# Block 0's second query half evicted by ScalarE, and block 14's last rows, a router product and a guard step in other places

## The chip, the cores and the metric

One core of one Trainium2 chip runs the whole kernel. The metric is device microseconds (us) of one launch. Five engines run beside each other and meet through semaphores: TensorE (PE in the profile) multiplies, VectorE (DVE) and ScalarE (ACT) read PSUM and write SBUF, GpSimd (POOL) works on SBUF and starts indirect DMAs, SyncE (SP) starts the other DMAs.

## The reference

Input x is 2048 tokens of 448 numbers (bfloat16). The first half is attention with 16 heads of 28 numbers, one shared key and one shared value head. The second half is a mixture-of-depths MLP: only the 8 tokens with the largest router value go through it.

```python
h  = x + attention(layernorm(x))        # q = xn @ wq (16 heads), k = xn @ wk, v = xn @ wv (one head)
                                        # softmax(q k^T / sqrt(28)) @ v, then @ wo
n  = layernorm(h)
r  = n @ w_r                            # router, one number per token
idx = argsort(-r)[:8]
y  = ((silu(n[idx] @ w_gate) * (n[idx] @ w_up)) @ w_down) * sigmoid(r[idx])
out = h + n;  out[idx] += y
```

## The kernel before

**Tiling.** Tokens are cut into 16 tiles of 128. A *block* b is a tile of 128 queries with all 16 heads, a *tile* j is 128 keys. For every pair (b, j) TensorE makes four strips of scores, 128 keys x 512 (query, head) pairs each. Of these 256 pairs, 169 go to ScalarE, which takes two strips in one `Exp` into `P` (`act_tile`, line 888; line 874 for the early tiles below, which are kept in the buffers of `wg_sb` and `wu_sb`). The other 87 go to VectorE (`dve_tile`, line 915): it clamps the scores to an int16 whose bits are an approximate exponential, `Y`, and GpSimd adds two constants to copies of it, `Yc` (line 926); three products with differently scaled values sum to the exponential. TensorE multiplies `P`, `Y` and `Yc` with the values into one PSUM bank, `ACC`, one block after the other (line 853). `_ND` is the number of VectorE tiles of each block (sum 87 before and after).

**Start.** `group(g)` handles one group of token tiles, `groups = [[0], [1], [2, 3], [4, 5], [6, 7], [8..11], [12..15]]`: layer norm statistics (lines 724 to 733), normalised rows `of` (ScalarE line 742 or VectorE lines 737 and 746), transposes to `xnT` (757, 762), keys `K` (772) and values `Vs` (785). Keys are wanted twice, in `K[:, 0]` and, shifted by 32 partitions, in `K[:, 1]`. For a group in `_KD` the second copy is made by two DMAs, for the others by a second VectorE instruction. `q_project(b)` makes the queries of a block: 16 matmuls, then an eviction that adds a one (line 803 on ScalarE, 806 on VectorE). Block 0 is evicted in two halves, the first by ScalarE, the second by VectorE. `_EARLY` lists positions inside block 0 at which three tiles of block 1 (keys 0, 1 and 2) are done ahead by ScalarE.

**After each block.** `evict(b)` copies `ACC` to `Ot` (953) and fetches the reciprocal of the row sums by way of DRAM (`l_scr`, `Rb`); `On` (966) is the normalised output; `out_proj(t)` multiplies by `wo` and adds x (`of`, 996), takes statistics (998, 999) and the router product `junk` (1001). `ln2` makes rstd on ScalarE with Ln and Exp (1012, 1014) and the output rows. Block 14 (`N1`) is alone in its `ln2` group; its router product is made there, with rstd already in it (line 1023), and its two row instructions run on ScalarE (1026 to `xn2`, 1030 to `of`).

**End.** `stage1` finds the best 8 tokens of each of the first 14 tiles and gathers those 112 rows by an indirect DMA (1127). `tail` finishes block 15 without DRAM: row sums by a shuffle (1156), reciprocal by Ln and Exp on ScalarE (1158, 1160) and `On` (1165), each in two halves; `last_rows` takes statistics (1041, 1042), rstd (1043, 1045), router product (1047), router value (1052) and rows (1058, 1060). Then: maximum and index over 368 candidates (1200, 1201), a one-hot `oh` (1208), the selected rows `xsel`, gate and up products, SiLU (1236 to 1244), down product, a gather of the 8 rows of the output (`base`, 1256), their sum `fin` (1264) and an indirect write (1267). A guard checks that all row sums lie in a sane interval (1276, 1278) and sets a flag that every engine waits for at the end; if it fails, an exact program runs.

**Order.** Each engine's order is made when the kernel is built: a list planner (`_Flow.plan`) goes over all instructions with a duration, a priority and their dependencies, and appends to each engine the one that can start soonest in its model, by priority within a window (`_WIN`). `_W`, `_LOOK`, `_LATE` and `_HOLD` are its settings; the duration in `G.op(engine, fn, duration)` is what the planner believes. On the chip the order of each engine is fixed and semaphores decide the times. `lock=True` keeps GpSimd's instructions from running beside a VectorE instruction.

Of the kernel before, what the change touches and what calls it, by code (L numbers as in the profile page):

```python
# [240 lines left out]
_KD = (1, 2, 4)  # L241
_EARLY = (0, 6, 9)
# [271 lines left out]
def _fast(nc, G, sb, ps, psb, flag, scr, rows, A_x, A_wq, A_wk, A_wv, A_wo, B_w_r, B_w_gate, B_w_up, B_w_down, out):  # L514
# [204 lines left out]
    def group(g):  # L719
# [29 lines left out]
        for a in range(t0, t1, 2):  # L749
            m = min(2, t1 - a)  # L750
            u = G.unit()

            def cut(a, ch):
                return 2 * (ch // 2) if a == 0 else 0

            def tr(k, ch, u=u, a=a, m=m):
                return lambda e: e.transpose(psb[0:CK, u.b[0], (ch * m + k) * 128:(ch * m + k + 1) * 128],  # L757
                                             of[:, a + k, ch * CK + cut(a, ch):(ch + 1) * CK + cut(a, ch)], ident[:, :])
            G.op(PE, [tr(k, ch) for k in range(m) for ch in range(NCH)], m * 4 * (150 if g == 0 else 80),
                 reads=[("of", a + k) for k in range(m)] + ["ident"], writes=[u.key], take=u)  # L760
            dst = xnT[0:CK, :, a * 128:(a + m) * 128]
            G.op(DV, lambda e, u=u, m=m, dst=dst: e.tensor_copy(
                dst, psb[0:CK, u.b[0], 0:NCH * m * 128].rearrange("p (c n) -> p c n", c=NCH)), 65 + m * 265,
                 reads=[u.key], writes=[("xnT", a + k) for k in range(m)], free=u)
# [26 lines left out]
    def q_project(b):  # L791
        war = G.readers.get(("Q", b % 3), [])
        for c in ((0, 2), (2, 4)) if b == 0 else ((0, 4),):
            u = G.unit()
            n = c[1] - c[0]
            for h in range(*c):
                G.op(PE, [mm(bank(u, c=slice((h - c[0]) * 128, (h - c[0] + 1) * 128)), wq_pad[0:CK, ch, h, :],
                             xnT[0:CK, ch, b * 128:(b + 1) * 128], ch == 0, ch == NCH - 1) for ch in range(NCH)], 470 if b == 0 else 430 if b == 1 else 235,
                     reads=[("wqp", ch) for ch in range(NCH)] + ["wq_pad", ("xnT", b)], writes=[u.key],
                     take=u if h == c[0] else None, after=war)  # L800
            src = lambda u=u, n=n: ps[:, u.b[0], 0:128 * n].rearrange("p (h n) -> p h n", n=128)
            if b == 0 and c[0] == 0:
                G.op(AC, lambda e, c=c, src=src: e.activation(Q[:, 0, c[0]:c[1], :], src(), ACT.Identity, bias=qone[:, 0:1]),
                     340, reads=[u.key, "qone"], writes=[("Qa", 0)], free=u)
            else:
                G.op(DV, lambda e, c=c, src=src: e.tensor_scalar(Q[:, b % 3, c[0]:c[1], :], src(), qone[:, 0:1], None, ALU.add),  # L806
                     60 + n * 150, reads=[u.key, "qone"], writes=[("Q", b % 3)], free=u)
# [200 lines left out]
    def ln2(ts):  # L1008
# [3 lines left out]
        G.op(AC, lambda e: e.activation(st[:, sl, 0], sv[:, :, 1], ACT.Ln, bias=ebias[:, 0:1]), 300,  # L1012
             reads=[("stf", t) for t in ts] + ["ebias"], writes=[("st0", t) for t in ts])
# [6 lines left out]
        for t in ts:  # L1020
            if t == N1:
                blk14.append(s3)
                G.op(DV, lambda e, t=t: e.scalar_tensor_tensor(junk[:, :], of[:, t, 0:D], st[:, t, 1:2], w_rb[:, :], ALU.mult,
                                                               ALU.mult, accum_out=st[:, t, 4:5]), 600,
                     reads=[("of", t), ("st1", t), "w_rb"], writes=["junk", ("st4", t)], lock=True)
                G.op(AC, lambda e, t=t: e.activation(xn2[:, 0, :], of[:, t, 0:D], ACT.Identity, bias=st[:, t, 3:4],
                                                     scale=st[:, t, 1:2]), 600,
                     reads=[("of", t), ("st1", t), ("st3", t)], writes=[("xn2", t)], prio=b_last,
                     after=G.readers.get(("xnT", NT - 1), []))
                G.op(AC, lambda e, t=t: e.activation(of[:, t, 0:D], of[:, t, 0:D], ACT.Identity, bias=st[:, t, 3:4],  # L1030
                                                     scale=st[:, t, 2:3]), 600,
                     reads=[("of", t), ("st2", t), ("st3", t)], writes=[("of", t)], prio=b_last)
# [7 lines left out]
    def last_rows(t, u, hp, stf):  # L1040
# [4 lines left out]
        G.op(AC, lambda e: e.activation(st[:, t, 1:2], st[:, t, 0:1], ACT.Exp, scale=-0.5), 200, reads=[("st0", t)],  # L1045
             writes=[("st1", t)])
# [102 lines left out]
    def tail():  # L1149
# [4 lines left out]
        for h in range(2):  # L1154
# [5 lines left out]
            G.op(AC, lambda e, sl=sl: e.activation(Rb[:, rb, sl], Rb[:, rb, sl], ACT.Exp,  # L1160
                                                       bias=-63.0 * math.log(2.0), scale=-1.0), 330,
                 reads=[("Rbh", h)], writes=[("Rbh", h)])
# [704 lines left out]
```

## Time and profile before

| | |
|---|---|
| median of 3 runs | 348.62 us (348.61 to 348.75) |
| profiled execution | 348.56 us |
| its span, first to last instruction | 346.6 us |
| outside the span | 1.96 us |
| busy PE / DVE / ACT / POOL | 318.2 / 319.4 / 325.4 / 190.8 us |
| first `Exp` of the scores starts, last one ends | 10.95 us, 326.93 us |

How to read it: three engines are busy over 90% of the span, so shares do not tell which one sets the end. Look at which engine has no idle time in a stage and whom the others wait for. In a timeline row the columns are start, length, engine, line, operation, output and input with shapes and count, and in brackets the idle time before it with what ended that time. Neighbouring instructions overlap by about 0.1 us in these lengths. Three stages matter: the start, until ScalarE has a full stream of `Exp` work (0 to 17 us), the stream (17 to 327 us), and the end (327 to 346.6 us).

### The profile page before, as it was taken

Reading aid. Unit: us, or ns where it says so; the run is one execution under the profiler, and the core shown is the slowest. Engines: PE = TensorE matmul, PEld = TensorE weight load, DVE = VectorE, ACT = ScalarE, POOL = GpSimd, SP = SyncE. Lnnn points to the kernel's source line nnn. Section 1 sums busy time; section 2 is a strip of 40 time slices with the busy share of each in tenths; the row PEclk is TensorE's granted clock in tenths of the full one; section 3 lists DMA queues with packets and bytes.
Section 4 is the critical chain, followed back from the end, with each engine's and each line's share of the span. In section 5 each row is a group of like instructions: output and inputs, shape, how many; then the busy total and the mean of one; then the engine's idle time right before and its main releaser. Section 6 shows DMA issues by size and latency. Waiting matters only on the chain.

```text
span 346.6 us, 8725 instructions
## 1 busy us (share of the span) xinstructions
PE 318.2 (92%) x3630; PEld 105.2 (30%) x3630; DVE 319.4 (92%) x662; ACT 325.4 (94%) x387; POOL 190.8 (55%) x206
## 2 busy tenths in 40 slices
PE   3889899999999999999999998999999999999974
PEld 2644232323232322323232322323232322222334
DVE  6998997999988999999899899999999899999874
ACT  5599999999999999999999999999999999999850
POOL 8010475666545648667456566576747456775401
PEclk9999999999999999999999999999999999999995
DMA  6510000000020205020020206020101012152210
GB/s 158 138 40 3 0 3 18 20 17 18 5 85 4 84 4 168 27 60 30 8 80 5 84 4 165 4 46 16 33 4 30 7 58 85 42 152 58 60 36 9
DMA packets 18374, 16.18 MB, mean 47 GB/s; under 512 B 6574, under 2 KB 15438, under 8 KB 18330
## 3 DMA queue, kind: packets, MB, share of 16 engines
q1 hardware_dynamic: 16826, 15.01, 15.5%
q8 instruction: 29, 0.48, 0.6%
q10 hardware_dynamic: 1392, 0.45, 0.6%
q0 software_dynamic: 112, 0.12, 0.1%
q14 instruction: 15, 0.12, 0.1%
HBM read 11.78 MB, written 3.71 MB: 45 GB/s over the span
## 4 chain that ended last, share of the span: by engine, by line
ACT 83%; DVE 9%; DMA 3%; PE 3%; issue 0%; POOLq 0%; POOL 0%; ACTq 0%; DVEq 0%
ACT P L888 80%; DVE Y L915 4%; PE ps L628 2%; DMA wqx<-in_A_wq_dram 1%; ACT wg_sb L874 1%; DMA wqx<-n_rows,cidx 1%; DVE bn L724 1%; PE ps L823 1%; DMA cidx<-gidx 1%; ACT wu_sb L874 1%; DVE K L772 0%; ACT wqx L711 0%; DVE Q L806 0%; PE ps L757 0%; DVE gidx L1123 0%
## 5 line engine op out<-in xcount | busy, mean ns | idle before, releaser
L888 ACT ACTIVATE P<-ps 128x1024 bf16<-128x1024 f32 x332 | 306.8, 1287 | 0.0
L926 POOL INT64_ADD Yc<-Y x174 | 178.5, 1037 | 127.7 <-DVE Y L915 112.3
L915 DVE TENSOR_SCALAR Y<-ps 128x512 int16<-128x512 f32 x348 | 220.0, 683 | 12.0 <-PE ps L823 11.3
L823 PE MATMUL ps<-Q,K 32*128 32x512 bf16 (+1 forms) x1024 | 147.1, 386 | 14.1 <-ACT P L888 10.8
L823 PEld LDWEIGHTS ps<-Q,K 32*128 32x128 bf16 (+1 forms) x1024 | 37.7, 91 | 142.9 <-ACT P L888 122.1
L853 PE MATMUL ps<-Yc,Vs 128*32 128x512 bf16 x696 | 63.9, 385 | 0.0
L853 PE MATMUL ps<-P,Vs 128*32 128x512 bf16 x664 | 59.4, 387 | 0.0
L853 PE MATMUL ps<-Y,Vs 128*32 128x512 bf16 x348 | 34.2, 384 | 0.2 <-DVE Ot L953 0.2
L853 PEld LDWEIGHTS ps<-P,Vs 128*32 128x32 bf16 x664 | 14.1, 93 | 28.3 <-issue 26.2
L853 PEld LDWEIGHTS ps<-Yc,Vs 128*32 128x32 bf16 x696 | 15.7, 94 | 21.5 <-issue 15.8
L628 PE MATMUL ps<-xnT,wqx 112*128 112x128 bf16 x256 | 21.6, 229 | 0.0
L628 PE MATMUL ps<-wo_pad,On 128*32 128x448 bf16 (+1 forms) x244 | 18.1, 358 | 1.2 <-DVE Y L915 0.6
L628 PEld LDWEIGHTS ps<-xnT,wqx 112*128 112x128 bf16 x256 | 15.6, 102 | 7.7 <-issue 4.8
L806 DVE TENSOR_SCALAR Q<-ps,qone 128x512 bf16<-128x512 f32 (+1 forms) x16 | 11.6, 727 | 1.0 <-PE ps L628 0.9
L853 PEld LDWEIGHTS ps<-Y,Vs 128*32 128x32 bf16 x348 | 9.1, 94 | 9.3 <-issue 7.4
L966 DVE TENSOR_TENSOR On<-Ot,Rb 128x512 bf16<-128x512 f32 x15 | 11.0, 734 | 0.5 <-DMA Rb<-l_scr 0.5
L757 PE MATMUL ps<-ident,of 128*112 128x128 bf16 x64 | 6.3, 248 | 5.5 <-DVE of L737 5.5
L996 DVE TENSOR_TENSOR of<-ps,x_sb 128x448 bf16<-128x448 f32 x15 | 9.3, 619 | 1.1 <-PE ps L628 1.1
L953 DVE COPY Ot<-ps 128x512 f32<-128x512 f32 x15 | 10.3, 685 | 0.0
L724 DVE BATCH_NORM_STATS2 bn<-x_sb 128x6 f32<-128x448 bf16 x16 | 9.5, 610 | 0.0
L998 DVE BATCH_NORM_STATS2 bn<-of 128x6 f32<-128x448 bf16 x15 | 9.3, 622 | 0.1
L1001 DVE SCALAR_TENSOR_TENSOR junk<-of,w_rb 128x448 bf16<-128x448 bf16 x14 | 8.5, 611 | 0.0
(169 smaller groups left out, 141.4 us busy)
## 6 DMA issues: line engine op xcount, KB each, us to landing
Rb<-l_scr SPq DMA_DIRECT2D x15, 256.0 KB
out_dram<-of SPq DMA_DIRECT2D x16, 112.0 KB, 2.2
n_rows<-of SPq DMA_DIRECT2D x14, 113.0 KB, 2.4
x_sb<-in_A_x_dram SPq DMA_DIRECT2D x3, 448.0 KB, 4.4
wg_sb<-in_B_w_gate_dram SPq DMA_DIRECT2D x3, 448.0 KB, 6.1
wu_sb<-in_B_w_up_dram SPq DMA_DIRECT2D x3, 448.0 KB, 6.1
xnT<-in_B_w_down_dram SPq DMA_DIRECT2D x3, 448.0 KB, 7.7
wqx<-in_A_wq_dram ACTq DMA_DIRECT2D x1, 392.0 KB, 4.6
```

The source lines that it names most:

```text
L628: return lambda e: e.matmul(o() if callable(o) else o, lhsT=l, rhs=r, start=start, stop=stop)
L724: G.op(DV, lambda e, t=t: e.bn_stats(bn6[:, t, :], x_sb[:, t, :]), 516, reads=[("x", t)], writes=[("bn6", t)], after=[G.last_w[("xnT", 0)] ...
L806: G.op(DV, lambda e, c=c, src=src: e.tensor_scalar(Q[:, b % 3, c[0]:c[1], :], src(), qone[:, 0:1], None, ALU.add), 60 + n * 150, reads=[u. ...
L823: return e.matmul(ps[:, u.b[0] + q, :], lhsT=K[a:a + w, i % 2, j * 128:(j + 1) * 128], rhs=Q[a:a + w, b % 3, :, :].rearrange("p h n -> p ( ...
L853: return e.matmul(ps[32 * i:32 * i + 32, ACC, :], lhsT=Vs[:, v, j, :], rhs=src(i), start=info["first"] == o.idx, stop=info["last"] == o.idx)
L888: G.op(AC, lambda e, u=u, p=p, n=n: e.activation(P[:, p:p + n, :], ps[:, u.b[0]:u.b[0] + n, :], ACT.Exp, bias=EB, scale=OCT), 50.0 + 426.5 ...
L915: G.op(DV, lambda e, u=u, g0=g0: e.tensor_scalar(Y0[:, g0, :].bitcast(I16), ps[:, u.b[0], :], 0.0, TOP - STEP[-1], ALU.max, ALU.min), 599, ...
L926: G.op(PO, lambda e: e.int64_add(Yc[:, c, :, :].rearrange("p a b -> p (a b)").bitcast(I64), Y0[:, 4 * s:4 * s + 4, :].rearrange("p a b -> ...
L953: o = G.op(DV, lambda e: e.tensor_copy(Ot[:, rb, :], ps[:, ACC, :]), 598, reads=[pk(ACC)], writes=[("Ot", rb)], prio=b - 10.0, after=blk[b ...
L966: G.op(DV, lambda e: e.tensor_tensor(On[:, rb, :, :].rearrange("p h n -> p (h n)"), Ot[:, rb, :], Rb[:, rb, :], ALU.mult), 599, reads=[("O ...
L996: G.op(DV, lambda e: e.tensor_tensor(of[:, t, 0:D], hp(), x_sb[:, t, :], ALU.add), 535, reads=[u.key, ("x", t)], writes=[("of", t)], free=u)
L998: G.op(DV, lambda e: e.bn_stats(bn6[:, t, :], of[:, t, 0:D]), 520, reads=[("of", t)], writes=[("bn6", t)])
```

## The change

1. In block 0 both halves of the queries are evicted by ScalarE (line 803); before, the second one went to VectorE (806).
2. `_KD` goes from groups 1, 2, 4 to groups 2, 4, 5: the shifted keys of tile 1 are written by VectorE, those of tiles 8 to 11 by DMA. `_EARLY` goes from positions 0, 6, 9 to 0, 0, 6.
3. Block 14's router product becomes the ordinary one of `out_proj` (line 1001, without rstd), and a small VectorE instruction in `tail` multiplies by rstd afterwards. Block 14's Ln (1012) must now follow the last Exp of block 15's reciprocal (1160), and block 14's two row instructions (1026, 1030) must follow block 15's rstd (1045). These are orders on ScalarE alone.
4. The second half of the guard over block 15's sums (1278) must follow the last gate product, `guT` of half 1 (1244).
5. The index addition (1123) is locked against GpSimd.
6. The planner believes shorter TensorE times in the start (transposes 100 instead of 150, key matmul 75 instead of 145, a head's query projection 235 instead of 470 or 430 ns), its settings differ, and the split of tiles between ScalarE and VectorE differs by block.

```diff
-_KD = (1, 2, 4)
-_EARLY = (0, 6, 9)
+_KD = (2, 4, 5)
+_EARLY = (0, 0, 6)
...
-_ND = (2, 7, 6, 3, 7, 7, 6, 5, 5, 7, 6, 5, 4, 5, 6, 6)
+_ND = (2, 6, 6, 4, 6, 7, 6, 5, 6, 7, 4, 5, 8, 4, 6, 5)
...
-_LOOK = 111.5
-_WIN = {PE: 19.3, AC: 9.3, DV: 14.5, PO: 615.1, SP: 1.0}
-_LATE = (4, 113.8)
+_LOOK = 264.5
+_WIN = {PE: 11.7, AC: 35.3, DV: 13.7, PO: 7.8, SP: 1.0}
+_LATE = (4, 136.0)
...
-_HOLD = {'A': 11.2, 'D': 224.6}
+_HOLD = {'A': 9.9, 'D': 252.0}
...
-            G.op(PE, [tr(k, ch) ...], m * 4 * (150 if g == 0 else 80),
+            G.op(PE, [tr(k, ch) ...], m * 4 * (100 if g == 0 else 80),
...
-                  for ch in range(NCH)], 4 * (145 if g == 0 else 5 + w / 2.4), ...
+                  for ch in range(NCH)], 4 * (75 if g == 0 else 5 + w / 2.4), ...
...
-                             ... for ch in range(NCH)], 470 if b == 0 else 430 if b == 1 else 235,
+                             ... for ch in range(NCH)], 235,
...
-            if b == 0 and c[0] == 0:
+            if b == 0:
                 G.op(AC, lambda e, ...: e.activation(Q[:, 0, c[0]:c[1], :], src(), ACT.Identity, bias=qone[:, 0:1]),
-                     340, reads=[u.key, "qone"], writes=[("Qa", 0)], free=u)
+                     340, reads=[u.key, "qone"], writes=[("Qa" if c[0] == 0 else "Q", 0)], free=u)
...
-        if t != N1:
-            G.op(DV, ... junk ... accum_out=st[:, t, 4:5]), 600,
+        G.op(DV, ... junk ... accum_out=st[:, t, 4:5]), 540,
...
             if t == N1:
                 blk14.append(s3)
-                G.op(DV, lambda e, t=t: e.scalar_tensor_tensor(junk[:, :], of[:, t, 0:D], st[:, t, 1:2], w_rb[:, :], ...
-                G.op(AC, ... xn2[:, 0, :] ...)
-                G.op(AC, ... of[:, t, 0:D] ...)
+                late14.append(ln)
+                late15.append(G.op(AC, ... xn2[:, 0, :] ...))
+                late15.append(G.op(AC, ... of[:, t, 0:D] ...))
...
-        G.op(AC, ... st[:, t, 1:2], st[:, t, 0:1], ACT.Exp, scale=-0.5), 200, ...        # last_rows, block 15
+        q = G.op(AC, ... st[:, t, 1:2], st[:, t, 0:1], ACT.Exp, scale=-0.5), 200, ...
+        for o in late15:
+            o.deps[q.idx] = False
...
-            G.op(AC, ... Rb[:, rb, sl], Rb[:, rb, sl], ACT.Exp, ...                       # tail
+            q = G.op(AC, ... Rb[:, rb, sl], Rb[:, rb, sl], ACT.Exp, ...
+        for o in late14:
+            o.deps[q.idx] = False
...
-        G.op(DV, ... gidx ... ALU.add), 70, reads=["idx1", "base1f"], writes=["gidx"])
+        G.op(DV, ... gidx ... ALU.add), 100, reads=["idx1", "base1f"], writes=["gidx"], lock=True)
...
-        G.op(DV, lambda e: e.scalar_tensor_tensor(rp[:, N1:N1 + 1], st[:, N1, 3:4], sw[:, 0:1], st[:, N1, 4:5], ...
+        G.op(DV, lambda e: e.tensor_scalar(st[:, N1, 5:6], st[:, N1, 4:5], st[:, N1, 1:2], None, ALU.mult), 62, ...
+        G.op(DV, lambda e: e.scalar_tensor_tensor(rp[:, N1:N1 + 1], st[:, N1, 3:4], sw[:, 0:1], st[:, N1, 5:6], ...
...
+            n_ = G.last_w[("guT", 1)][0]
...
-                 writes=["okj", ("okc", n)], ..., lock=True)
+                 writes=["okj", ("okc", n)], ..., lock=True, after=[] if n == 0 else [n_])
```

More of the change, by code (lines that the diff above doesn't have):

```diff
@@ L758, in tr @@
                                              of[:, a + k, ch * CK + cut(a, ch):(ch + 1) * CK + cut(a, ch)], ident[:, :])
-            G.op(PE, [tr(k, ch) for k in range(m) for ch in range(NCH)], m * 4 * (150 if g == 0 else 80),
+            G.op(PE, [tr(k, ch) for k in range(m) for ch in range(NCH)], m * 4 * (100 if g == 0 else 80),
                  reads=[("of", a + k) for k in range(m)] + ["ident"], writes=[u.key], take=u)
@@ L768, in group @@
         G.op(PE, [mm(bank(uk, c=slice(0, w)), wk_rep[0:CK, ch, :], xnT[0:CK, ch, sl], ch == 0, ch == NCH - 1)
-                  for ch in range(NCH)], 4 * (145 if g == 0 else 5 + w / 2.4), reads=[("wkr", r) for r in range(4)] + ["wk_rep"] + [("xnT", t) for t in tl_],
+                  for ch in range(NCH)], 4 * (75 if g == 0 else 5 + w / 2.4), reads=[("wkr", r) for r in range(4)] + ["wk_rep"] + [("xnT", t) for t in tl_],
              writes=[uk.key], take=uk)
@@ L797, in q_project @@
                 G.op(PE, [mm(bank(u, c=slice((h - c[0]) * 128, (h - c[0] + 1) * 128)), wq_pad[0:CK, ch, h, :],
-                             xnT[0:CK, ch, b * 128:(b + 1) * 128], ch == 0, ch == NCH - 1) for ch in range(NCH)], 470 if b == 0 else 430 if b == 1 else 235,
+                             xnT[0:CK, ch, b * 128:(b + 1) * 128], ch == 0, ch == NCH - 1) for ch in range(NCH)], 235,
                      reads=[("wqp", ch) for ch in range(NCH)] + ["wq_pad", ("xnT", b)], writes=[u.key],
@@ L1011, in ln2 @@
         sv = of[:, sl, D:RW].bitcast(F32)
-        G.op(AC, lambda e: e.activation(st[:, sl, 0], sv[:, :, 1], ACT.Ln, bias=ebias[:, 0:1]), 300,
-             reads=[("stf", t) for t in ts] + ["ebias"], writes=[("st0", t) for t in ts])
+        ln = G.op(AC, lambda e: e.activation(st[:, sl, 0], sv[:, :, 1], ACT.Ln, bias=ebias[:, 0:1]), 300,
+                  reads=[("stf", t) for t in ts] + ["ebias"], writes=[("st0", t) for t in ts])
         G.op(AC, lambda e: e.activation(st[:, sl, 1], st[:, sl, 0], ACT.Exp, scale=-0.5), 100, reads=[("st0", t) for t in ts],
@@ L1022, in ln2 @@
                 blk14.append(s3)
[L1023 to L1032, printed above, removed]
+                late14.append(ln)
+                late15.append(G.op(AC, lambda e, t=t: e.activation(xn2[:, 0, :], of[:, t, 0:D], ACT.Identity,
+                                                                   bias=st[:, t, 3:4], scale=st[:, t, 1:2]), 600,
+                                   reads=[("of", t), ("st1", t), ("st3", t)], writes=[("xn2", t)], prio=b_last,
+                                   after=G.readers.get(("xnT", NT - 1), [])))
+                late15.append(G.op(AC, lambda e, t=t: e.activation(of[:, t, 0:D], of[:, t, 0:D], ACT.Identity,
+                                                                   bias=st[:, t, 3:4], scale=st[:, t, 2:3]), 600,
+                                   reads=[("of", t), ("st2", t), ("st3", t)], writes=[("of", t)], prio=b_last))
             else:
@@ L1044, in last_rows @@
              writes=[("st0", t)])
-        G.op(AC, lambda e: e.activation(st[:, t, 1:2], st[:, t, 0:1], ACT.Exp, scale=-0.5), 200, reads=[("st0", t)],
-             writes=[("st1", t)])
+        q = G.op(AC, lambda e: e.activation(st[:, t, 1:2], st[:, t, 0:1], ACT.Exp, scale=-0.5), 200, reads=[("st0", t)],
+                 writes=[("st1", t)])
+        for o in late15:
+            o.deps[q.idx] = False
         G.op(DV, lambda e: e.scalar_tensor_tensor(junk[:, :], hp(), 1.0, w_rb[:, :], ALU.mult, ALU.mult,
@@ L1159, in tail @@
                  writes=[("Rbh", h), ("Rb", rb)])
[L1160 removed]
+            q = G.op(AC, lambda e, sl=sl: e.activation(Rb[:, rb, sl], Rb[:, rb, sl], ACT.Exp,
                                                        bias=-63.0 * math.log(2.0), scale=-1.0), 330,
[L1162 removed]
+                     reads=[("Rbh", h)], writes=[("Rbh", h)])
+        for o in late14:
+            o.deps[q.idx] = False
         for h in range(2):
```

24 lines of the change are left out of this document (14 added, 10 removed).

## The prediction

> **What bounds the kernel now.** I read the page first, then the windows, the waits in the stream, and the timelines of the start and the end.
>
> ```profile
> span 346.6 us, 8725 instructions
> ACT 83%; DVE 9%; DMA 3%; PE 3%; issue 0%; POOLq 0%; POOL 0%; ACTq 0%; DVEq 0%
> L888 ACT ACTIVATE P<-ps 128x1024 bf16<-128x1024 f32 x332 | 306.8, 1287 | 0.0
> L915 DVE TENSOR_SCALAR Y<-ps 128x512 int16<-128x512 f32 x348 | 220.0, 683 | 12.0 <-PE ps L823 11.3
> ...
> 260.00:300.00 40.00, 38.12 (x433) 10.33 (x425) 37.85 (x73) 40.00 (x47) 24.57 (x24) 1.00 0.13 39
> ...
> ACT wg_sb L874 <- PE ps L823: 0.6, 1, 0.6
> PE ps L823 <- ACT P L888: 10.8, 45, 0.6
> DVE Y L915 <- PE ps L823: 11.3, 35, 0.8
> ```
>
> The chain that ended last runs 83% on ScalarE. In a late window its busy time (fourth pair) is 40.00 of 40.00 us, and from 16.9 to 325 us its only wait is 0.6 us at the very start. The score matmuls wait 10.8 us for it, VectorE waits 11.3 us for them. So in the stream ScalarE is the bound and the two others have about 11 us to spare each. One `Exp` costs 306.8 / 332 = 0.924 us net (the mean of 1287 ns overlaps the next one); one strip on VectorE 220.0 / 348 = 0.632 us. The change leaves 87 VectorE tiles and 338 `Exp` (169 tiles, two each), so the stream's work is unchanged. Time can be won only before the stream, where ScalarE is idle, and after it.
>
> **The start.** ScalarE, VectorE, SyncE and TensorE, each from its own timeline or its tile's view:
>
> ```profile
> 10.28 0.76 ACT L742 ACTIVATE of<-x_sb,nb,rstd 128x448 bf16<-128x448 bf16 x1 [0.43 <-DVE nb L733]
> 10.95 2.06 ACT L888 ACTIVATE P<-ps 128x1024 bf16<-128x1024 f32 x2
> 14.52 0.30 ACT L728 ACTIVATE var<-mv,ebias 128x2 f32<-128x2 f32 x1 [1.52 <-DVE mv L726]
> ...
> 15.81 0.30 ACT L728 ACTIVATE var<-mv,ebias 128x2 f32<-128x2 f32 x1 [0.75 <-DVE mv L726]
> ...
> 16.89 1.94 ACT L874 ACTIVATE wg_sb<-ps 128x1024 bf16<-128x1024 f32 x2 [0.55 <-PE ps L823]
> ```
> ```profile
> 9.70 0.47 DVE L806 TENSOR_SCALAR Q<-ps,qone 128x256 bf16<-128x256 f32 x1
> ...
> 11.54 0.40 DVE L772 TENSOR_SCALAR K<-ps,kcol 128x128 bf16<-128x128 f32 x1
> ...
> 15.69 0.72 DVE L806 TENSOR_SCALAR Q<-ps,qone 128x512 bf16<-128x512 f32 x1
> ...
> 29.19 1.52 DVE L772 TENSOR_SCALAR K<-ps,kcol 128x512 bf16<-128x512 f32 x2
> ```
> ```profile
> 11.97 1.27 SPq L640 DMA_DIRECT2D K<-K  x2
> ...
> DMA to landing us min/median/max: 1.7/1.8/3.0
> ```
> ```profile
> 7.21 1.86 PE L628 MATMUL ps<-xnT,wqx 112*128 112x128 bf16 x16
> ...
> 10.23 0.61 PE L823 MATMUL ps<-Q,K 64*128 64x512 bf16 x2 [0.56 <-DVE nb L733]
> ...
> 14.61 1.28 PE L628 MATMUL ps<-xnT,wqx 112*128 112x128 bf16 x20
> ...
> 7.20:9.07 1.87, 1.87 (x21) 1.83 (x20) 1.00 0.28 69
> ```
>
> After the two `Exp` of tile 0 ScalarE has almost nothing until 16.89: idle 1.52 + 0.75 + 0.55 = 2.82 us. Tile 1 cannot be scored there, because its shifted keys come by DMA: keys at 11.54 + 0.40, two issues in 1.27, landing 1.7 to 3.0 later, so 13.7 to 16.2. The next work is the early tile of block 1, which waits for block 1's queries (VectorE, 15.69).
>
> **Change, part by part.**
>
> *`_KD`, group 1.* The shifted keys of tile 1 become one VectorE instruction of 0.40. They are there by about 12.4 instead of 13.7 to 16.2, and two SyncE issues go. Tile 1's scores (0.61 a pair) and two `Exp` (1.85) fit right behind tile 0's, which end at 13.01. At least these 1.85 us move into the hole; at most the whole idle 2.82 goes. I take 2.3: two more early tiles follow at once (`_EARLY` 0, 0), but they still need block 1's queries, whose 16 matmuls and 0.72 eviction leave part of the hole open. What is late next is that eviction.
>
> *Block 0's second query half.* The matmuls end at 7.21 + 1.86 = 9.07; VectorE only comes at 9.70 and is done at 10.17, and the scores start at 10.23. ScalarE could do it right at 9.07, some 0.48 us long, so scores could be 0.6 earlier. But the first `Exp` starts at 10.95 because ScalarE is normalising tile 2 until then, and this waits for an rstd that now queues behind the eviction, up to 0.25 later. Bounds: 0.6 won, 0.25 lost; I take 0, nearest to the row that ends at 10.95. VectorE loses 0.47 and gains tile 1's 0.40: nothing.
>
> *`_KD`, group 5.* VectorE saves half of 1.52, 0.76 us, where it has slack: 0 gained. Tiles 8 to 11 now need two issues (about 0.6 each) and a landing: 29.19 + 0.76 + 1.2 + 1.8 to 3.0 = 33.0 to 34.2, against 30.7 before. With ScalarE 2.3 ahead and one early tile more in front of tile 8, that tile is wanted about 33. Bounds 0 to 1.0 us of waiting, I take 0.2. The issues are in front of nothing on SyncE but block 0's row sums, which come much later.
>
> *`_ND` and the settings.* Same totals; taken at 0, hidden by the 11 us that TensorE and VectorE have spare. If that cover is gone it costs as in the third and fourth rivals.
>
> **The end.** Timeline of ScalarE and VectorE, then the other engines, and a step of the chain:
>
> ```profile
> 314.72 12.21 ACT L888 ACTIVATE P<-ps 128x1024 bf16<-128x1024 f32 x13
> ...
> 329.30 0.28 ACT L1012 ACTIVATE st<-of,ebias 128x1 f32<-128x1 f32 x1
> 329.49 0.40 ACT L1160 ACTIVATE Rb<-Rb 128x256 f32<-128x256 f32 x1
> ...
> 331.28 0.75 ACT L1026 ACTIVATE xnT<-of,st 128x448 bf16<-128x448 bf16 x1
> 332.06 0.76 ACT L1030 ACTIVATE of<-of,st 128x448 bf16<-128x448 bf16 x1
> 332.73 0.28 ACT L1043 ACTIVATE st<-of,ebias 128x1 f32<-128x1 f32 x1
> 333.05 0.20 ACT L1045 ACTIVATE st<-st 128x1 f32<-128x1 f32 x1
> ```
> ```profile
> 329.93 0.42 DVE L1165 TENSOR_TENSOR On<-ps,Rb 128x256 bf16<-128x256 f32 x1 [0.49 <-ACT Rb L1160]
> ...
> 330.39 0.68 DVE L1023 SCALAR_TENSOR_TENSOR junk<-of,st,w_rb 128x448 bf16<-128x448 bf16 x1
> ...
> 331.73 0.18 DVE L1042 BATCH_NORM_AGGREGATE of<-bn 128x2 f32<-128x6 f32 x1
> ...
> 332.33 0.21 DVE L1050 TENSOR_SCALAR st<-of,sw 128x1 f32<-128x1 f32 x1
> ...
> 333.28 0.28 DVE L1052 TENSOR_SCALAR rp<-st 128x1 bf16<-128x1 f32 x1 [0.67 <-ACT st L1045]
> ```
> ```profile
> 327.36 3.46 DMA wqx<-n_rows,cidx
> ```
> ```profile
> 339.65 1.78 PE L628 MATMUL ps<-guT,xnT 128*128 128x8 bf16 x56
> ```
> ```profile
> base<-out_dram,tok POOLq DMA_INDIRECT x1, 3.8
> ...
> 337.82 0.89 POOL L1256 DMA_INDIRECT base<-out_dram,tok  x1 [9.32 <-DVE tok L1254]
> ...
> 342.27 0.67 DVE L1264 TENSOR_TENSOR fin<-ps,base 8x256 bf16<-8x256 f32 x2 [0.30 <-PE ps L628]
> ```
>
> *Block 14's rows behind block 15's rstd.* Block 15's variance is there at 331.73 + 0.18 = 331.91, but its Ln starts at 332.73, behind the two rows of block 14. With the new order it starts at about 332.0 and rstd is done 0.75 earlier. The router value (333.28) waited 0.67 for it; its other input is made at 332.33 to 332.54, so it gains 0.73. What ScalarE could wait for instead is the gather of candidates (landing 330.82, then 0.5 of small instructions): a cover of some 0.65 before it delays block 15's Ln.
>
> *Block 14's Ln behind the reciprocal.* It stood for 0.19 in front of the last Exp (329.30 to 329.49), and `On` waited for that: up to 0.19 won. Block 14's product (0.61 net) must now go elsewhere on VectorE. It stood in the wait for TensorE; the place nearest is the idle 0.49 before 329.93, which it overfills by 0.12. Net 0 to 0.19, I take 0.1. The extra VectorE instruction beside `rp` lies in a wait, 0.
>
> *Guard.* The down products run on TensorE from 339.65 for 1.78, half of which covers what half 1's gate product needs: 0 gained. Moved, the 0.63 of guard lies beside the second half of them. *Index addition locked:* the gather may start some 0.7 earlier, and is off the path when rstd no longer stands behind it: 0.
>
> *What is late next.* The gather of `base` lands at 337.82 + 3.8 = 341.62 and `fin` starts at 342.27: 0.65 spare. It needs all output rows in DRAM. ScalarE still does four row instructions after the rstd, so the last of them ends at about the same time as before, and its transfer does not move. The end therefore gains 0.7 of the 0.83, bounds 0.3 and 1.3 (the upper one if `Rb` of block 14 lands early enough to take block 14's VectorE work, three instructions, out of the end).
>
> **Sum.** Start 2.3 + end 0.7 - group 5's wait 0.2 = 2.8 us. The profiled execution took 348.56 (span 346.6 and 1.96 around it), 0.06 under the median of 348.62. 348.56 - 2.8 = 345.8. Bounds of this case: 2.82 + 0.6 + 1.3 = 4.7 won, 343.9; 1.85 - 0.25 - 1.0 + 0.3 = 0.9 won, 347.7.
>
> [...] TensorE's matmuls of 128 columns took 1.86 / 16 = 116 ns at 7.21 and 1.28 / 20 = 64 ns at 14.61, while the granted clock is given as 1.00 (third number from the right of the window row). The planner now counts 235 ns for a head of four matmuls that took 465.
> [...]
>
> **The rivals.**
> - *The start's order doesn't fit the real TensorE.* If block 1's 16 projections stand ahead of tile 1's scores because they are thought to take 0.94 and take 1.86, tile 1's `Exp` come 0.92 later than they could. The start wins 1.4: 348.56 - 1.4 - 0.7 + 0.2 = 346.7. Against it: keys of tile 1 and queries of block 0 are ready before. Chance 0.14.
> - *No change.* ScalarE starts its stream earlier and runs into the others: keys of group 5 (1.0 late) and bank waits give back 1.5 more, and the base gather holds the end. About 348.4, between 347.9 and 349.3. For it: TensorE is busy 38.12 of 40 us. Against it: both others wait some 11 us in all for ScalarE's pace. Chance 0.13.
> - *Slower.* Block 12 gets 8 VectorE tiles: 32 strips of 0.632 = 20.2 us against 8 x 2 x 0.924 = 14.8 on ScalarE, 5.4 us too much for one block. Blocks 11 and 13 (5 and 4 tiles) and `P`, which holds 8 tiles, must take it up. If they don't, ScalarE idles 5.4 us there: 348.56 - 2.8 + 5.4 = 351.2. It decides from 3.5 us of idle on. Before, blocks 4 and 5 with 7 each were taken up without a wait. Chance 0.12.
>
> **Numbers.** The forecast has 0.61. Faster by over 0.2% (0.7 us, about what a measurement tells from no change): 0.61 + 0.14 = 0.75. Same 0.13, slower 0.12. The range is 344.0 to 349.0: it leaves out the slower rival and the rim of the rest. The likeliest case alone gives 343.9 to 347.7.
>
> **What would show it.** Right: `Exp` of tile 1 from about 13.0; idle between 13 and 17 under 1 us; the last `Exp` near 324.6 instead of 326.93; between it and the end of the span 19.0 instead of 19.67; block 15's Ln right behind its variance. Wrong: ScalarE waits longer than 0.6 us in the stream, above all in block 12 or for keys near 33 us; the last `Exp` not earlier; `fin` waiting for `base`; Ln of block 15 behind the candidate gather.

## The result and the profile after

| | before | after |
|---|---|---|
| median | 348.62 us (348.24 to 348.75, 4 runs) | 362.57 us (362.02 to 362.99, 4 runs) |
| ratio, 95% interval | | 1.0401 [1.0383, 1.0419] |
| profiled execution, its span | 348.56, 346.6 us | 362.99, 360.9 us |
| first `Exp` starts | 10.95 | 24.14 |
| first early tile (`wg_sb`) starts | 16.89 | 29.93 |
| last `Exp` ends | 326.93 | 341.40 |
| from there to the end of the span | 19.67 | 19.50 |

The change is slower by 14 us. Of the 14.3 us by which the span grew, 13.04 are there when the first early tile starts; the stream adds 1.43, the end gives back 0.17. The page after (span, shares of the chain, and the costliest wait of a matmul group, whose last column is idle time and its releaser):

```profile
span 360.9 us, 8735 instructions
...
ACT 84%; PE 7%; issue 4%; DVE 2%; POOL 2%; POOLq 0%; DVEq 0%
...
L758 PE MATMUL ps<-ident,of 128*112 128x128 bf16 x64 | 6.0, 247 | 16.5 <-POOL ident L673 16.0
```

The chain has 4% of "issue", which it had not before, and TensorE's first transposes wait 16.0 us for GpSimd's `ident`. That points at GpSimd's timeline of the start, which the prediction shows nowhere. Before:

```profile
0.82 0.10 POOL L666 MEMSET one<- 128x2 f32 x1 [0.29 <-POOLq L1852]
1.07 0.18 POOL L667 INT64_ADD one<-one  x1
1.20 0.09 POOL L668 MEMSET ebias<- 128x1 f32 x1
1.25 0.28 POOL L670 TENSOR_SCALAR_AFFINE_SELECT tri<-idi 128x128 bf16<-128x128 bf16 x1
1.50 0.28 POOL L672 TENSOR_SCALAR_AFFINE_SELECT ident<-idi 128x128 bf16<-128x128 bf16 x1
```

After, with ScalarE's and TensorE's rows that hang on it:

```profile
0.85 0.09 POOL L668 MEMSET ebias<- 128x1 f32 x1
9.32 0.28 POOL L671 TENSOR_SCALAR_AFFINE_SELECT tri<-idi 128x128 bf16<-128x128 bf16 x1 [8.38 <-issue]
15.50 0.18 POOL L667 INT64_ADD one<-one  x1 [5.89 <-issue]
15.65 0.28 POOL L673 TENSOR_SCALAR_AFFINE_SELECT ident<-idi 128x128 bf16<-128x128 bf16 x1
```
```profile
15.99 0.68 PE L758 MATMUL ps<-ident,of 128*112 128x128 bf16 x4 [15.99 <-POOL ident L673]
...
20.93 1.87 PE L628 MATMUL ps<-xnT,wqx 112*128 112x128 bf16 x16 [3.04 <-POOL wqx L715]
```
```profile
10.30 0.85 ACT L706 ACTIVATE wk_rep<-wk_sb 112x112 bf16<-112x112 bf16 x4 [6.66 <-DVE iota L1082]
...
24.14 1.00 ACT L889 ACTIVATE P<-ps 128x1024 bf16<-128x1024 f32 x1
...
29.93 1.02 ACT L875 ACTIVATE wg_sb<-ps 128x1024 bf16<-128x1024 f32 x1 [3.22 <-PE ps L824]
```

GpSimd does the same five instructions in another order: `tri` stands ahead of INT64_ADD. Two waits appear, 8.38 and 5.89 us, and both end with "issue": no semaphore ended them. Ahead of each wait GpSimd's sequencer has a pair of MODIFY_POOL_CONFIG, at 1.0 us (L671) and at 9.8 us (L667). Before, one such pair stands among the five, at 0.9 to 1.0 us, and INT64_ADD follows it at 1.07. The expectations below call such a wait a load of code: that is the author's reading, the trace shows the pair and the wait. The planner made this order because GpSimd's window went from 615.1 to 7.8 in the settings (a run below changes that alone). VectorE's third instruction is a sum over `tri`, so nearly its whole start waits too; the 6.66 in ScalarE's row is a wait for VectorE.

Why the first wait is 2.49 us longer than the second, no run here shows.

### The profile page after: what moved, and what is told of

It reads as the page before. It is cut to its first block, busy times and chain, and to the rows that moved or that the text cites. A ratio compares the mean times of both kernels' runs of the same rounds, so it can differ in the third digit from the quotient of the medians.

```text
span 360.9 us, 8735 instructions
## 1 busy us (share of the span) xinstructions
PE 317.1 (88%) x3630; PEld 103.9 (29%) x3630; DVE 319.7 (89%) x662; ACT 325.0 (90%) x388; POOL 191.0 (53%) x206
## 4 chain that ended last, share of the span: by engine, by line
ACT 84%; PE 7%; issue 4%; DVE 2%; POOL 2%; POOLq 0%; DVEq 0%
ACT P L889 82%; PE ps L628 4%; PE ps L824 1%; PE ps L854 1%; PE ps L758 1%; ACT wg_sb L875 1%; POOL K L698 0%; POOL Vs L699 0%; POOL wqx L715 0%; DVE Ot L1158 0%; ACT xnT L1060 0%; ACT st L1014 0%; POOL out_dram L1273 0%; ACT of L1030 0%; DVE bn L1041 0%
## 5 line engine op out<-in xcount | busy, mean ns | idle before, releaser
L824 PE MATMUL ps<-Q,K 32*128 32x512 bf16 (+1 forms) x1024 | 144.2, 387 | 15.5 <-ACT P L889 12.9
L824 PEld LDWEIGHTS ps<-Q,K 32*128 32x128 bf16 (+1 forms) x1024 | 36.3, 91 | 144.8 <-ACT P L889 127.5
L854 PE MATMUL ps<-Yc,Vs 128*32 128x512 bf16 x696 | 64.7, 384 | 0.0
L854 PE MATMUL ps<-P,Vs 128*32 128x512 bf16 x664 | 62.0, 395 | 1.2 <-ACT P L889 0.9
L807 DVE TENSOR_SCALAR Q<-ps,qone 128x512 bf16<-128x512 f32 x15 | 11.1, 742 | 1.1 <-PE ps L628 1.1
L758 PEld LDWEIGHTS ps<-ident,of 128*112 128x112 bf16 x64 | 5.0, 150 | 18.7 <-POOL ident L673 16.0
```

Source lines behind the costliest of these rows:

```text
L824: return e.matmul(ps[:, u.b[0] + q, :], lhsT=K[a:a + w, i % 2, j * 128:(j + 1) * 128], rhs=Q[a:a + w, b % 3, :, :].rearrange("p h n -> p ( ...
L854: return e.matmul(ps[32 * i:32 * i + 32, ACC, :], lhsT=Vs[:, v, j, :], rhs=src(i), start=info["first"] == o.idx, stop=info["last"] == o.idx)
```

## The experiments

Two questions: are GpSimd's two waits the whole of the loss, and why does the rest of the change not win its 2.8 us?

| kernel | median us | ratio to before, 95% |
|---|---|---|
| change, INT64_ADD first | 349.54 | 1.0022 [1.0007, 1.0038] |
| before, `tri` first | 360.99 | 1.0359 [1.0343, 1.0375] |
| change, GpSimd's window 615.1 | 349.43 | 1.0024 [1.0012, 1.0036] |
| change, INT64_ADD late | 359.34 (one run) | |
| before, `iota` near the end | 355.81 | 1.0215 [1.0202, 1.0228] |
| before, second query half on ScalarE | 348.83 | 1.0005 [0.9995, 1.0015] |
| before, tile 1 first | 349.70 | 1.0030 [1.0014, 1.0045] |
| change, tile 1 ahead of early tiles | 359.71 | 1.0306 [1.0273, 1.0339] |
| before, block 15's rstd first | 348.60 | 1.0000 [0.9991, 1.0009] |
| the same, TensorE's stream shifted | 349.00 | 1.0016 [1.0007, 1.0025] |
| before, 34 products at the start | 348.19 | 0.9994 [0.9985, 1.0003] |
| change (INT64_ADD first), 34 products | 347.40 | 0.9978 [0.9956, 0.9999] |
| the same, TensorE's waits filled | 346.39 | 0.9949 [0.9933, 0.9964] |
| the same, filled beyond the waits | 346.56 | 0.9942 [0.9929, 0.9955] |
| before, 34 products and waits filled | 347.41 | 0.9971 [0.9961, 0.9981] |

### GpSimd's two waits

**Change with INT64_ADD first.** The finished order is edited, all other engines keep theirs:

```diff
+ for lst in (orders[PO], seq):
+     lst.remove(first["int64"]); lst.insert(lst.index(first["tri"]), first["int64"])
```


> The changed kernel with one edit: after planning, GpSimd's first INT64_ADD (line 667) is put in front of its first affine select (the triangle), as the kernel before has it; every other engine keeps the changed kernel's order. [...] Gone: 8.38 + 5.89 = 14.3 us, so 362.57 - 14.3 = 348.3 or a little less, 346 to 348.5 if the first prediction's steps hold in part (first forecast 345.8). [...] Rival B (the plan itself is slow): start at the usual time, but the stream and the end lose; 350 or more.

349.54: 13 of the 14 us are gone, `ident` is at 1.50 again.

**Before with `tri` first.** The same edit, one place behind `tri`, in the kernel before.

> The kernel before with one edit: INT64_ADD moved behind the first affine select in GpSimd's order, nothing else. Code loading: the two waits of 8.4 and 5.9 us appear here too, 348.62 + 13 to 14.5 = 361.6 to 363. Rival A: the same order of waits as in the kernel before, no change, 348.6. Rival B: no change, 348.6, because the plan of the changed kernel is to blame.

360.99. The same two waits in a kernel that has nothing else of the change:

```profile
9.86 0.28 POOL L674 TENSOR_SCALAR_AFFINE_SELECT tri<-idi 128x128 bf16<-128x128 bf16 x1 [8.91 <-issue]
16.05 0.18 POOL L671 INT64_ADD one<-one  x1 [5.91 <-issue]
```

**Only GpSimd's window set back.**

```diff
-_WIN = {PE: 11.7, AC: 35.3, DV: 13.7, PO: 7.8, SP: 1.0}
+_WIN = {PE: 11.7, AC: 35.3, DV: 13.7, PO: 615.1, SP: 1.0}
```


> The changed kernel with only the planner's window of GpSimd set back from 7.8 to 615.1; the planner then puts INT64_ADD first by itself and orders the rest anew. If the window is what let the select pass, 346 to 349; code loading gone as in the run with INT64_ADD put first. Rival B: 350 or more.

349.43, the same as the first edit: one number of the settings is the cause. With 615.1 the planner puts INT64_ADD first by itself.

**INT64_ADD just ahead of the first `Yc` instead.**

> The changed kernel with INT64_ADD moved from between the two affine selects to right in front of GpSimd's first copy of the stream (line 927), some 20 us later. Code loading: one wait of 8.4 us before the first select stays, the one of 5.9 us moves to where GpSimd waits for VectorE anyway: 362.6 - 5.9 = 356.7, or 355 to 358. Rival A: the waits are tied to the time, not to the instruction: 362.6.

359.34 (one run), 3.2 us better than the change; the forecast was wrong by 2.6.

```profile
9.50 0.28 POOL L675 TENSOR_SCALAR_AFFINE_SELECT tri<-idi 128x128 bf16<-128x128 bf16 x1 [8.57 <-issue]
9.75 0.28 POOL L677 TENSOR_SCALAR_AFFINE_SELECT ident<-idi 128x128 bf16<-128x128 bf16 x1
```
```profile
15.17 0.64 PE L762 MATMUL ps<-ident,of 128*112 128x128 bf16 x4 [15.17 <-DVE of L742]
```

`ident` is 5.9 earlier, the transposes only 0.8: they now wait for VectorE's normalised rows. Here and in the change (first and second line):

```profile
12.61 2.41 DVE L742 TENSOR_SCALAR of<-x_sb,mv,rstd 128x448 bf16<-128x448 bf16 x1 [0.60 <-ACT rstd L735]
12.44 0.40 DVE L738 TENSOR_SCALAR of<-x_sb,mv,rstd 128x448 bf16<-128x448 bf16 x1 [0.60 <-ACT rstd L731]
```

VectorE was held by `tri` in both; but here its instruction took 2.41 instead of 0.40. GpSimd's fills and its copy of `wqx` ran beside it, where in the change GpSimd stood still. That they slow it is the author's estimate from 2.41 against 0.40; no run tests it. In the change this copy comes only behind the second wait, and the query products wait 3.04 for it (20.93, above). Here they start at 16.89, 4.04 earlier, and the early tile at 25.88 instead of 29.93. With INT64_ADD first it starts at 16.75. So of the 13.18 us between 29.93 and 16.75 the first wait accounts for 9.13 (with the 2.0 of the slow instruction in it), and moving the second out of the start won 4.05. The end of this run is 0.8 longer than the change's, which takes a part back.

**Why before has no such wait.** An `iota` (128x1, read by nobody) behind the gather of candidates, where GpSimd is idle for 9.3 us:

```diff
+ G.op(PO, lambda e: e.iota(pidx[:, :], [[0, 1]], base=0, channel_multiplier=1), 1, writes=["pidx"], ...)
```


> The kernel before with one GpSimd iota (128x1, its result read by nobody) behind the gather of the candidates at 328.5 us, where GpSimd has 9.3 us of nothing to do; the listing shows a load of code ahead of it. Theory: what code GpSimd holds lasts from one launch to the next, so the load ahead of INT64_ADD at 1.07 us costs nothing only because INT64_ADD's code was the last one used; with iota's code left behind, INT64_ADD waits 5.9 us for issue at the start, ident comes at about 7.5 us instead of 1.50, the first transposes 2 to 3 us later: 351 us (350.3 to 352.5). Rival: the first load of a launch is always hidden ahead of the span: no such wait, 348.6, or up to 0.5 more if the iota's own load meets the gather of base at 337.8.

355.81. In the profiled launch, start and end:

```profile
7.79 0.18 POOL L667 INT64_ADD one<-one  x1 [6.90 <-issue]
```
```profile
342.41 0.13 POOL L1130 IOTA pidx<- 128x1 int32 x1 [6.74 <-issue]
344.32 1.11 POOL L1256 DMA_INDIRECT base<-out_dram,tok  x1 [1.78 <-DVE tok L1254]
```

At the end the wait of 6.74 is hidden: the gather of `base` waits 1.78 for `tok` after it. The start pays 6.90, with the order of before untouched. So what GpSimd ran at the end of one launch decided what the next one waited for. In both kernels the first GpSimd instruction of a launch behind the fills is INT64_ADD; the last of a launch, but for indirect DMAs, is INT64_ADD before (`Yc`, 324.45) and the `iota` here. The size was missed: I expected the transposes 2 to 3 us later, but `tri` holds VectorE, so its normalised rows start 6.14 later, and with GpSimd's fills beside them they take 1.32 instead of 0.40. The transposes came at 12.56 instead of 5.50, and that 7.1 is the loss of 7.3.

### The start

**Second query half on ScalarE**, alone, in the order of before:

> The kernel before in its own order, with block 0's second query half moved from VectorE to ScalarE, right behind the first. The prediction's step says 0, bounds 0.6 won and 0.25 lost: 348.5, first Exp still near 10.95 us. Rival: scores come 0.6 earlier and so does the stream, 347.9. Rival: the rstd behind it comes 0.25 later and shifts all: 348.8.

348.83, no measurable change, as forecast; the first `Exp` starts at 10.88 instead of 10.95.

**Tile 1 first**, alone, planned anew:

```diff
-_KD = (1, 2, 4)
-_EARLY = (0, 6, 9)
+_KD = (2, 4, 5)
+_EARLY = (1, 6, 9)
```


> The kernel before with _KD (2, 4, 5) and _EARLY (1, 6, 9), planned anew: tile 1 of block 0 no longer waits for a DMA and is written ahead of the early tile. Written order: two Exp fill the hole between 13 and 16.9 us, 348.54 - 1.85 = 346.7, between 345.8 and 347.6. Rival (TensorE in the start): hole as before, 348.5. A new plan of the rest may move either by some 0.3 us.

349.70, not faster. Tile 1's `Exp` do come behind tile 0's, but the early tile then starts at 18.18 instead of 16.89, and 2.1 us of small waits for scores follow (timeline, then the waits after 20 us). Two of the five waits (0.39 and 0.49, near 41 and 43 us) stand where the granted clock was 0.50, and the ten executions differ in this: the four with a mean clock of 0.980 or less took 350.18 to 351.14 (the profiled one 350.85), the six from 0.984 on 348.79 to 349.81.

```profile
13.62 1.94 ACT L888 ACTIVATE P<-ps 128x1024 bf16<-128x1024 f32 x2 [0.66 <-PE ps L823]
...
18.18 1.94 ACT L874 ACTIVATE wg_sb<-ps 128x1024 bf16<-128x1024 f32 x2 [1.17 <-PE ps L823]
```
```profile
ACT P L888 <- PE ps L823: 2.1, 5, 0.5
```

**Tile 1 ahead of the early tiles in the change** (`_EARLY` (1, 1, 6), INT64_ADD first, planned anew):

> The changed kernel with INT64_ADD first and one number pair more: _EARLY (1, 1, 6) instead of (0, 0, 6), so that tile 1 of block 0 is written ahead of the two early tiles of block 1; planned anew. Theory (written order): ScalarE's score pairs are chained in the order in which the tiles are written, so with 0, 0 the early tiles, which wait for block 1's queries, stand in front of tile 1, and the hole of 3.2 us behind tile 0 stays. With 1, 1 two Exp (1.85 us) move into it: 349.54 - 1.85 = 347.7, between 346.8 and 348.5, and ScalarE's wait for the early tile's scores falls from 3.2 to under 1.5 us. Rival (TensorE in the start): the 16 projections at half speed hold tile 1's scores as well, the hole stays at 3 us, 349.5.

359.71, a clear miss. Tile 1's `Exp` starts at 16.11 after 2.67 of waiting for scores, hardly sooner than the early tile did in the edit with INT64_ADD first (16.75). Still, ScalarE's ninth `Exp` starts at 22.80 instead of about 23.65, so by then some 0.85 of the 1.85 is won. The new plan then loses it many times over: the last `Exp` ends 6.9 later than with INT64_ADD first (4.3 of it in two waits for the products with the values), and the end is 2.6 longer. The whole was planned anew, so the time of this run says little of tile 1's place.

In the change with INT64_ADD first the picture is this (ScalarE, then TensorE):

```profile
10.96 1.01 ACT L893 ACTIVATE P<-ps 128x1024 bf16<-128x1024 f32 x1
...
12.51 1.01 ACT L893 ACTIVATE P<-ps 128x1024 bf16<-128x1024 f32 x1
16.75 1.02 ACT L879 ACTIVATE wg_sb<-ps 128x1024 bf16<-128x1024 f32 x1 [3.22 <-PE ps L828]
```
```profile
12.90 1.87 PE L632 MATMUL ps<-xnT,wqx 112*128 112x128 bf16 x16
14.56 1.06 PE L762 MATMUL ps<-ident,of 128*112 128x128 bf16 x8
15.55 0.62 PE L858 MATMUL ps<-P,Vs 128*32 128x512 bf16 x4
16.10 1.04 PE L828 MATMUL ps<-Q,K 64*128 64x512 bf16 x4
```

Behind tile 0 comes not tile 1 but the early tile of block 1, which needs block 1's queries, and these 16 products take 117 ns each. TensorE has no gap between them and the scores at 16.10. ScalarE's hole is still there, as one wait of 3.22. The half pace lasts longer than before: the next products at full pace (12 in 0.83 us) stand at 18.15, in the kernel before (20 in 1.28) at 14.61.

**34 products of `ident` by `ident` ahead of TensorE's first transposes**, where it had nothing to do until 5.50; in the kernel before, and in the change with INT64_ADD first:

```diff
+ G.op(PE, [mm(ps[:, ACC, 0:128], ident[:, :], ident[:, :], True, True) for _ in range(34)], 1, reads=["ident"], ...)
```


> The kernel before in its own order on every engine, with 34 products of ident by ident (128x128 by 128x128, into the accumulator's bank, read by nobody) put ahead of TensorE's first transposes, which until 5.50 us had nothing to do. Theory: TensorE runs at half speed at the start because it has not yet been busy long enough, and what ScalarE waits for at 13 to 17 us is that half speed. The matmuls of the start (16 query products in 1.86 us, transposes at 105 ns) then take about half from some 6 to 7 us on, the hole of 2.8 us before the first early tile shrinks by 1 to 2 us: 347.2 us (346.5 to 348.0). Rival: the pace of the start is set by VectorE's and GpSimd's copies and by the loads, or the clock does not follow TensorE's work: 348.6, and 349 if the 34 products hold up the first transposes.

> The changed kernel with INT64_ADD first (349.54 us), with the same 34 products ahead of TensorE's first transposes. Theory: the change's start was planned for matmuls at full clock and meets a TensorE at half clock, for longer than before; ScalarE's wait of 3.22 us at 16.75 is made of that. With TensorE warm the wait falls to 1 to 2 us: 347.8 us (347.0 to 348.6), more won than in the kernel before. Rival: the wait is the chain of score pairs and the copies in front of it, not the clock: 349.5.

348.19 and 347.40: nothing measurable for the kernel before, 2.1 us for the change. TensorE's row and windows of the latter (length, busy and count of TensorE, granted clock, DMA):

```profile
7.37 1.07 PE L632 MATMUL ps<-xnT,wqx 112*128 112x128 bf16 x16 [0.34 <-ACT wqx L716]
```
```profile
6.00:9.00 3.00, 1.57 (x25) 1.00 0.77 237
9.30:12.00 2.70, 1.99 (x18) 0.50 0.71 191
12.00:16.00 4.00, 4.00 (x32) 0.50 0.22 62
16.20:19.00 2.80, 2.47 (x36) 1.00 0.02 6
```

With the 34 products ahead, block 0's 16 query products take 1.07 instead of 1.89, 67 ns each instead of 118. Behind 3 us in which TensorE was busy for 1.57 the granted clock fell to 0.50, from 9.18 to 16.01. The wait ahead of `wg_sb` was still 3.09; the first `Exp` and the early tile are about 1 us earlier (10.04 and 15.69). But the profiled execution is one of the long ones, 348.89. The twelve executions sort by their mean granted clock: the four from 0.986 on took 346.27 to 346.62, the eight of 0.981 or less 347.25 to 350.17 (the profiled one has 0.971, and its clock also fell to 0.50 near 146 us). That speaks for the clock, but only as a correlation; the next runs test it.

**The waits filled** with more of the same products (8, 5, 9, 3, 8 in the change; 9, 10, 6, 12 in the kernel before), and in the change once with 11, 8, 13, 5, 11:

> The changed kernel with INT64_ADD first and 34 products of ident ahead of the first transposes (347.4 us), with small groups of the same product where TensorE waited after that: 8 behind the first transposes, 5 behind the first V product, 9 behind the query products, 3 behind the first two score groups, 8 behind the next transposes. In the run without them the granted clock was 1.0 from 5.77 to 9.18 us only, 0.5 until 16.01, and 1.0 after that. Theory: the clock falls because TensorE waits for some 2 us in 5.8 to 9.2; with the waits filled it stays at 1.0, block 1's 16 query products (11.84 to 13.71) take 1.05 instead of 1.87, and ScalarE's wait of 3.09 us at 15.69 shrinks to about 1.5: 346.2 us (345.5 to 347.0). Rival: the clock falls all the same, or ScalarE's wait is then made by VectorE's copies: 347.4, or 347.8 if the fillers are in the way.

> As the one before, with 11, 8, 13, 5 and 11 products in the five places, some 15 in all more than the waits hold. Theory: what the clock needs is a TensorE that never waits; if the smaller groups are not enough these are, at 0.1 to 0.3 us of work held up: 346.4 us (345.7 to 347.2). Rival: each group that overruns its wait pushes the first Exp and all behind it back: 347.8.

> The kernel before with the 34 products at the start (348.19 us, no more than 0.1% won; clock 1.0 from 5.59 to 9.01, then 0.5 until 15.83) and groups of 9, 10, 6 and 12 of them in TensorE's waits at 5.9, 6.9, 8.5 and 9.7 us. Theory: as in the changed kernel the hole ahead of the early tile (idle 1.52, 1.10 and 0.56 us at 14.8 to 17.5) shrinks, here by about 1.3: 347.0 us (346.3 to 347.8). Rival: in the order before, what ends these waits is VectorE's statistics (the first two waits end with mv), so a warm TensorE is worth little: 348.1.

346.39 and 346.56 for the change: with 95% intervals wholly under 1, both beat the kernel before, and so the change with INT64_ADD first, whose interval is wholly above 1. 347.41 for the kernel before. The change, first filling: windows, TensorE, ScalarE.

```profile
6.00:9.00 3.00, 2.89 (x48) 1.00 0.79 236
9.30:12.00 2.70, 2.37 (x37) 1.00 0.72 208
12.00:16.00 4.00, 3.67 (x53) 1.00 0.22 60
```
```profile
11.47 1.05 PE L638 MATMUL ps<-xnT,wqx 112*128 112x128 bf16 x16
...
13.63 0.61 PE L834 MATMUL ps<-Q,K 64*128 64x512 bf16 x4 [0.33 <-DVE Q L817]
```
```profile
14.06 1.02 ACT L885 ACTIVATE wg_sb<-ps 128x1024 bf16<-128x1024 f32 x1 [1.38 <-PE ps L834]
```

Block 1's queries take 1.05 instead of 1.87, the early tile starts at 14.06 instead of 16.75, the last `Exp` ends at 324.57 (325.95 less the 1.38 waited there) instead of 327.85. In the kernel before the same filling wins 1.1; its hole is then ended by VectorE's statistics twice (1.07 and 0.75 us). By the medians the rest of the change is worth 1.0 us once both start warm, and costs 1.0 where TensorE starts cold (by the ratios 0.8 each).

### The end

**Block 15's rstd first**, alone, in the order of before:

> The kernel before in its own order, with one move: block 14's two row instructions (and the transfer of the second) behind block 15's Ln and Exp on ScalarE. The prediction's step says that rstd of block 15 comes 0.75 earlier and the router value 0.73 earlier, with the gather of base as the next limit: 0.7 won, 348.54 - 0.7 = 347.8. Rival (given back later): the router value is earlier, but the products behind it, or base, take it back: 348.3 to 348.6.

348.60, nothing won. Block 15's Ln starts 0.76 earlier, as the prediction had it, the router value 0.59 (0.73 predicted) and the gate products 0.60. Then TensorE stops (its up products before, then its timeline here):

```profile
338.14 1.63 PE L628 MATMUL ps<-xsel,wu_sb 128*128 128x8 bf16 x56
```
```profile
336.14 1.54 PE L638 MATMUL ps<-xsel,wg_sb 128*128 128x8 bf16 x56
337.54 1.33 PE L638 MATMUL ps<-xsel,wu_sb 128*128 128x8 bf16 x47
339.08 0.40 PE L638 MATMUL ps<-xsel,wu_sb 128*128 128x8 bf16 x9 [0.20 <-issue]
339.59 1.77 PE L638 MATMUL ps<-guT,xnT 128*128 128x8 bf16 x56
```

The down products start at 339.59 instead of 339.65: 0.54 of the 0.60 is given back. No semaphore ended the stop.

**TensorE's stream shifted.** 123 products of 1x1 at the start, to move the boundaries of its instruction blocks (in the trace of before 29 packets of 16 KB in queue q8, in the median 129 recorded matmuls apart):

> The kernel with block 15's rstd first (348.6 us where 348.0 was due; TensorE stopped for 0.37 us after its 3559th matmul, amid the up products), with 123 products of 1x1 by 1x1 ahead of TensorE's first transposes. TensorE's instructions arrive in blocks of 16 KB, one for every 128 matmuls. Theory: the stop belongs to such a boundary; 123 matmuls more in front put it among the five filling matmuls at 333.5 us, where TensorE waits anyway: up products in 1.55 us or less without a gap, 348.1 us (347.9 to 348.3). Rival: the stop belongs to the place in the work or to the clock's fall at 338.6: the gap stays at the same up product and the time at 348.6.

349.00, the up products took 1.94. The test was badly sized: with a boundary about every 128 matmuls, 123 more put the next boundary only 5 products later. The filled kernels settle it. They shift the stream by 67 and 71, and their blocks land at 334.97 (change) and 336.19 (before), with none from 336 to 338 and from 336.5 to 339.5; the stop stays in the up products:

```profile
335.45 1.31 PE L638 MATMUL ps<-xsel,wu_sb 128*128 128x8 bf16 x43
336.91 0.50 PE L638 MATMUL ps<-xsel,wu_sb 128*128 128x8 bf16 x13 [0.16 <-issue]
```
```profile
336.44 0.67 PE L635 MATMUL ps<-xsel,wu_sb 128*128 128x8 bf16 x21
337.35 1.06 PE L635 MATMUL ps<-xsel,wu_sb 128*128 128x8 bf16 x35 [0.25 <-issue]
```

So it is not the boundary. Without any products added the place differs too: after 47 up products here, after 21 with the query half on ScalarE. The second of the filled kernels has the order of before at the end, so the stop is not made by the edit either; the profiled execution of before is the one that shows none (its up products take 1.63, those of the sixteen other profiles 1.93 to 1.98). What the stop is, and with it where the 0.6 goes, stays open.

## Why the prediction was wrong

- **The step that failed: "`_ND` and the settings. Same totals; taken at 0."** Totals were the same and no cover of TensorE's or VectorE's was lost, but the settings fix an order, and GpSimd's was looked at nowhere. The diff showed `PO` from 615.1 to 7.8. The order of two GpSimd instructions costs 13 us; no rival had it, and the range ended at 349.0.
- **Tile 1 behind tile 0's `Exp`, 1.85 to 2.82 won, 2.3 taken.** Wrong in mechanism. In the order built, the early tile comes first and needs block 1's queries. The prediction named those queries as what is late next and still let tile 1 pass them. Where tile 1 was put first in the change, its `Exp` still waited 2.67 for TensorE; in the kernel before they fitted (13.62) and won nothing. With GpSimd's waits gone the hole was one wait of 3.22 and the early tile 0.14 earlier than before, 16.75 against 16.89.
- **The cold-TensorE rival** (0.14, 346.7) had the right cause and too small a price: the start won nothing by it, not 1.4. With the clock kept up the last `Exp` ends at 324.57, 2.36 earlier than before; the prediction had asked for about 324.6. The traces show the pace: before, the query products at 7.21 take 116 ns each and those at 14.61 take 64; with 34 products from 1.83 us on in the change, these take 3.81 us, 112 ns each, and the query products at 7.37 take 67. At how much work the pace changes, no run shows. The filled kernels put a price on it, 3.1 us for the change by the medians (2.5 by the ratios).
- **The stream.** Right that ScalarE bounds it and that block 12's 8 VectorE tiles cost nothing: between the early tile and the last `Exp` the filled change has no wait of ScalarE. Missed: two pairs of small Ln and Exp, which stood in the hole before, now stand in the stream. It is 310.51 long instead of 310.04 (311.10 with INT64_ADD first and no filling, where ScalarE waits 0.53 for scores at 21.81).
- **The query half, 0.** Held, as far as the interval tells (0.9995 to 1.0015).
- **The end, 0.7.** The first half held (Ln 0.76, gate products 0.60 earlier in the single edit). The step "what is late next" failed: it looked for a DMA, and in the profile the time was lost in TensorE's up products, with the cause open. In the filled change the end takes 19.73 (344.3 less 324.57), with INT64_ADD first 19.55, in the change 19.50, before 19.67: nowhere 0.7 less.
- **Group 5's keys by DMA, 0.2 lost.** Not seen: no such wait.

## What to carry to other kernels

When settings of a planner change, compare the order of every engine, the idle ones first: an engine off the critical path can hold the start (here GpSimd, by 13 us). Look for waits that end with "issue" and for what the engine ran ahead of them, in this launch or in the one before: here that decided between 0 and 5.89 to 6.90 us ahead of INT64_ADD. And try an order planned for a warm TensorE (here 64 to 67 ns for a product of 128 columns) with TensorE warm and cold (116 to 118 ns): this one won 1.0 us in the first case and lost 1.0 in the second. Idle time at the start was spent on products that nobody reads; 34 of them alone gave 347.40, with a clock of 0.50 again from 9.18 on, and with the gaps behind them filled too it was 346.39.

## What the hardware showed that was not expected

- GpSimd stood still, with no semaphore to end it, for 8.38 to 8.91 us ahead of the first affine select, 5.89 to 6.90 ahead of INT64_ADD and 6.74 ahead of `iota`; in the kernel before, where INT64_ADD is the first of a launch behind the fills and the last but for indirect DMAs, it came at 1.07 us without a wait.
- VectorE's normalised rows (128x448) took 0.40 us in the change, with GpSimd at rest, and 1.32 and 2.41 in two runs where GpSimd's fills and copies ran beside them.
- The clock fell in mid-stream. In the change it was 0.50 for 3.4 us, behind a stretch in which TensorE was busy for 3.08 of 4.00 us; ScalarE waited 0.65 for scores there:

```profile
155.00:159.00 4.00, 3.08 (x33) 1.00 0.00 0
159.50:162.90 3.40, 3.40 (x30) 0.50 0.04 7
```

- In the starts of the kernels without added products this column says 1.00 while products of 128 columns take 116 ns; the pace of a known product is the better witness there.
- TensorE's stop in the up products, which makes them some 0.3 us longer in sixteen of seventeen profiles; its cause is open.
